# Out-projection of an RWKV block: eight block products per unit, or seven with sums of activations on VectorE

## The chip, the cores and the metric

The kernel runs on one NeuronCore of a Trainium2 chip. Five engines have queues of their own: TensorE (PE; its weight loads are listed as PEld), VectorE (DVE), ScalarE (ACT), GpSimd (POOL) and SyncE (SP), which here only issues transfers. The metric is device time of the core in microseconds, as the median of several runs.

## The reference

The first part is a linear attention with a decaying state, for 4 batches, 8 heads, 768 tokens and head dimension 48. The second part is a feed-forward block on the 3072 tokens with 384 features.

```python
for t in range(S):
    kt, vt, rt, wt = (k[:, :, t], v[:, :, t], r[:, :, t], w[:, :, t])
    cur = np.einsum('bhd,bhe->bhde', u[None] * kt, vt)
    y[:, :, t] = np.einsum('bhd,bhde->bhe', rt, state + cur)
    state = wt[:, :, :, None] * state + np.einsum('bhd,bhe->bhde', kt, vt)
x = attn_out.transpose(0, 2, 1, 3).reshape(B * S, H * D)      # 3072 x 384
h = x @ w_in                                                  # 3072 x 2048
sp = np.maximum(h, 0.0) + np.log1p(np.exp(-np.abs(h)))
g = h * erf(sp)
return (g @ w_out).astype(np.float32)                         # 3072 x 384
```

All of it is fp32.

## The kernel before

The 3072 tokens are cut into 12 units of 256 tokens (NJ = 2 blocks of C = 128 tokens, from two batches). One step of the main loop does the attention of one unit and, between its parts, feed-forward work of earlier units. A unit goes through four stages: attention in step s, the hidden products in step s + 1 (`hidden`, L742), softplus, erf and the product h x erf on ScalarE and VectorE (L724, L727, L731), and the out-projection three steps after its attention (`project`, L771).

The hidden layer of a unit lies in two tiles h (the two halves of the 2048 features), each of 128 partitions x 8 feature blocks x 256 tokens. In `project` each feature block of 128 x 128 is the stationary operand and the 384 columns of w_out are the moving one: 16 feature blocks x 2 token blocks = 32 matmuls of 384 columns per unit. Both token blocks' sums lie in PSUM tiles m from a pool of two (`ps_m`), which the hidden products use too. ScalarE copies each finished sum (L780), and SP sends it out (L781).

Attention inside a step works by levels. At level n the products of neighbouring stretches of 2^(n-1) tokens are taken (`level_products`, L444), VectorE puts them into `own` (L456 and L418), and r and k are scaled by the running decays (`scale`, L260). The first four steps do all levels this way. From step DIRECT = 4 on, distances within blocks of 16 tokens are taken elementwise instead: `prepare` of the next step multiplies shifted rows of r, k and w ("terms", L374, L378, L393) and sums them (L364). VectorE does distances 0 to 4, GpSimd the others (both have L374 and L378). Those steps run `attend_late`, and only the products of the two highest levels are left to PE, at its start and after `place(1)`.

The order of work is written out by hand: every engine runs its instructions in the order of the program. `place(n)` inside the attention calls `in_order`, which takes pieces by letters: P is a piece of the out-projection of unit s - 3, H a piece of the hidden products of unit s - 1, A the next activation (`advance`).

```python
order = ("APPPAPP", "APPP", "HH", "AHHH", "AHHH", "PPAPP")
if s == DIRECT:
    order = ("APPP", "APPP", "APPHH", "AHHH", "AHHH")
```

In a step of `attend_late` the sequence is: level-5 products, scaling and take; the rest of the step before (`from_own`, `through_state`, L478 and L504); the first two parts of `prepare(s + 1)`; the product of kT with its decays (L586); `place(0)`; the next part of `prepare`, and so on. After the last step there remain the out-projections of units 9 to 11 and the hidden products of unit 11.

The weights come as 64-bit numbers and are turned into fp32 in the first three steps and the beginning of the fourth (`convert`): raw words land in tiles `words`, ScalarE splits them, VectorE shifts and joins (L217, L225), GpSimd adds the low part (L229). The same pool `words` later holds rows of r and k (`load_rows`, L178) and part of the terms; `rest` holds rows of w.

Of the kernel before, what the change touches and what calls it, by code (L numbers as in the profile page):

```python
# [11 lines left out]
FP32 = mybir.dt.float32  # L12
I32 = mybir.dt.int32
U32 = mybir.dt.uint32
AF = mybir.ActivationFunctionType
ALU = mybir.AluOpType

P = 128
# [3 lines left out]
NJ = 2  # L22
# [18 lines left out]
NEAR = 1 << NEAR_LOG  # L41
LOG = 6
MASKED = 5


def view(ap, offset, dims):
# [14 lines left out]
def kernel(  # L61
# [30 lines left out]
    const = ctx.enter_context(tc.tile_pool(name="const", bufs=1))  # L92
    ins = ctx.enter_context(tc.tile_pool(name="ins", bufs=2))
    att = ctx.enter_context(tc.tile_pool(name="att", bufs=2))
    xs = ctx.enter_context(tc.tile_pool(name="xs", bufs=3))
    hid = ctx.enter_context(tc.tile_pool(name="hid", bufs=4))
    act = ctx.enter_context(tc.tile_pool(name="act", bufs=2))
    wide = ctx.enter_context(tc.tile_pool(name="wide", bufs=4))
    outs = ctx.enter_context(tc.tile_pool(name="outs", bufs=2))
    dram = ctx.enter_context(tc.tile_pool(name="dram", bufs=2, space=bass.MemoryType.DRAM))  # L100
    ps_p = ctx.enter_context(tc.tile_pool(name="ps_p", bufs=1, space=PSUM))
    ps_y = ctx.enter_context(tc.tile_pool(name="ps_y", bufs=1, space=PSUM))
# [18 lines left out]
    u_row = const.tile([P, D], FP32, name="u_row")  # L121
    w_in_sb = const.tile([P, NT, DM], FP32, name="w_in_sb")
    w_out_sb = const.tile([P, NT, DM], FP32, name="w_out_sb")
    y = ps_y.tile([P, NE, NJ, NP // 2, C], FP32, name="y")

    turns = {"next": 0, "converting": False}
# [44 lines left out]

    def load_rows(s):

        rk = wide.tile([P, 2, DM, 2], I32, name="words", bufs=3)
        rk = rk[:].rearrange("p x n two -> p x (n two)").bitcast(FP32)
        w = wide.tile([P, 2, DM], I32, name="rest", bufs=2)
        w = w[:].rearrange("p x n -> p (x n)").bitcast(FP32)
        nc.sync.dma_start(out=rk, in_=rk_rows[s])  # L178
        nc.sync.dma_start(out=w, in_=w_rows[s])
        rows_of[s] = [x.rearrange("p (t n) -> p t n", t=NEAR) for x in (rk[:, 0], rk[:, 1], w)]  # L180

    def convert(weights):

        held = {}

        def load(i):
            if i >= len(weights):
                return  # L190
            dst, src = weights[i]
            if src.dtype == FP32:
                nc.sync.dma_start(out=dst, in_=src)
                return
            words = wide.tile([P, 2, DM, 2], I32, name="words", bufs=3)
            nc.sync.dma_start(
                out=words[:].rearrange("p i n two -> p i (n two)"), in_=src.bitcast(I32)
            )
            held[i] = [words]

        def scale(i):
            if i in held:
                words = held[i][0]
                low, high = words[:, :, :, 0], words[:, :, :, 1]
                base = ps_p.tile([P, 2, NP * C], FP32, name="pp1")[:, :, :DM]
                rest = wide.tile([P, 2, DM], I32, name="rest", bufs=2)


                nc.scalar.mul(out=base, in_=high.bitcast(FP32), mul=2.0**-112)

                nc.scalar.mul(out=rest[:], in_=low.bitcast(U32), mul=2.0**-29)
                held[i] += [base.bitcast(I32), rest]

        def shift(i):
            if i in held:
                bits = held[i][1]
                nc.vector.tensor_scalar(  # L217
                    out=bits, in0=bits, scalar1=3, scalar2=None, op0=ALU.logical_shift_left
                )

        def join(i):
            if i in held:
                words, bits, rest = held.pop(i)
                into = weights[i][0].bitcast(I32)
                nc.vector.scalar_tensor_tensor(  # L225
                    out=into, in0=words[:, :, :, 1], scalar=-(1 << 31), in1=bits,
                    op0=ALU.bitwise_and, op1=ALU.bitwise_or,
                )
                nc.gpsimd.tensor_tensor(out=into, in0=into, in1=rest[:], op=ALU.add)  # L229

        stages = {"l": load, "s": scale, "h": shift, "o": join}
        done = dict.fromkeys(stages, 0)
        for _ in range(3):
            load(done["l"])
            done["l"] += 1
        while True:
            what = yield
            for stage in {"j": "ho"}.get(what, what):
                stages[stage](done[stage])
                done[stage] += 1  # L240
            if weights[0][1].dtype != FP32:
                turns["converting"] = 0 < done["s"] and done["o"] < len(weights)
                turns["next"] = 0
# [20 lines left out]
    def prepare(s):  # L264
# [75 lines left out]
        r, k, w = rows_of.pop(s)  # L340
        k_rows = k
        front = att.tile([P, 2, JP, C], FP32, name="rk1", bufs=1)
        back = wide.tile([P, 2, DM, 2], I32, name="words", bufs=3)
        front = front[:].rearrange("p x n t -> p (x n t)")
        back = back[:].rearrange("p x n two -> p (x n two)").bitcast(FP32)
        terms, near = {}, 1 << near_log(s)
# [365 lines left out]

    later = []

    def hidden(xT, gs, cut):


        def activate(h):

            held = []  # L720

            def softplus():
                held.append(act.tile([P, FG, UNIT], FP32, name="sp"))
                nc.scalar.activation(held[0][:], h[:], AF.Softplus)  # L724

            def erf():
                nc.scalar.activation(held[0][:], held[0][:], AF.Erf)  # L727

            def multiply():
                for part in (slice(0, FG // 2), slice(FG // 2, FG)):  # L730
                    nc.vector.tensor_mul(h[:, part], h[:, part], held[0][:, part])  # L731

            later.extend([(softplus, True), (erf, True), (multiply, False)])

        for g in range(NG):
            h = hid.tile([P, FG, UNIT], FP32, name="h")
            gs.append(h)
            for f in range(0, FG, FT):
                ps = ps_m.tile([P, FT, UNIT], FP32, name="m")
                for ff in range(FT):  # L740
                    for kk in range(KT):
                        nc.tensor.matmul(  # L742
                            ps[:, ff, :],
                            lhsT=w_in_sb[:, g * FG + f + ff, kk * P : (kk + 1) * P],
                            rhs=xT[:, kk, :],
                            start=kk == 0,
                            stop=kk == KT - 1,
                        )
                    if cut and not ff and g == NG - 1 and f == FG - FT:
                        yield  # L750
                nc.scalar.copy(h[:, f : f + FT, :], ps[:])  # L751
                if f == FG - FT:
                    activate(h)
                yield

    def project(s, gs):

        c, i = divmod(s, SPC)
        ps = [None] * NJ

        halves = [slice(0, FG // 2), slice(FG // 2, FG)]
        for g in range(NG):
            for j, part in (
                [(j, part) for part in halves for j in range(NJ)]
                if not s and g == NG - 1
                else [(j, part) for j in range(NJ) for part in halves]
            ):
                if not g and not part.start:
                    ps[j] = ps_m.tile([P, DM], FP32, name="m")
                for f in range(FG)[part]:  # L770
                    nc.tensor.matmul(  # L771
                        ps[j][:],
                        lhsT=gs[g][:, f, j * C : (j + 1) * C],
                        rhs=w_out_sb[:, g * FG + f, :],
                        start=g + f == 0,
                        stop=g == NG - 1 and f == FG - 1,
                    )
                    if g == NG - 1 and f == FG - 1:
                        o = outs.tile([P, DM], FP32, name="o")
                        nc.scalar.copy(o[:], ps[j][:])  # L780
                        nc.sync.dma_start(out=out[i * NJ + j, c], in_=o[:])  # L781
                    if f % 4 == 3:
                        yield

    xTs, hids, projs = {}, {}, {}
    gated = [[] for _ in range(n_steps)]
# [19 lines left out]
    def piece(kind, of):  # L806
        if not 0 <= of < n_steps:
            return
        if of not in kind:
            kind[of] = hidden(xTs[of], gated[of], not of) if kind is hids else project(of, gated[of])  # L810
        next(kind[of])

    def in_order(s, k):


        order = ("APPPAPP", "APPP", "HH", "AHHH", "AHHH", "PPAPP")
        if s == DIRECT:
            order = ("APPP", "APPP", "APPHH", "AHHH", "AHHH")
        for what in order[k]:
# [27 lines left out]
    with tc.manual_schedule(  # L847
# [16 lines left out]
            ]  # L864
        )
        next(conversion)
        load_step(1)
        for s in range(n_steps):
            xTs[s] = xs.tile([P, KT, UNIT], FP32, name="xT")
# [5 lines left out]
                        conversion.send(what)  # L875

            def place(n):
                if n == (LOG - 1 if s <= DIRECT else 2) and DIRECT - 1 <= s < n_steps - 2:
                    load_rows(s + 2)
                for due in {(3, 4): (5,), (4, 3): (6,), (4, 5): (7,)}.get((s, n), ()):  # L880
                    load_w(due)
# [1 line left out]
                    load_w(s + 3)  # L883
                if s >= DIRECT:
                    in_order(s, next(places))
                    return
                if s in ALONE:
                    if s == 2 and not n:

# [131 lines left out]
```

## Time and profile before

| | |
|---|---|
| median of 3 runs | 616.82 us (616.64 to 618.1) |
| profiled execution, span from first to last instruction | 614.9 us |
| PE busy | 602.1 us (98%) |
| DVE busy | 409.3 us (67%) |
| ACT busy | 293.9 us (48%) |
| POOL busy | 293.3 us (48%) |
| out-projection L771 on PE | 252.1 us |
| hidden products L742 on PE | 257.3 us |
| mean granted TensorE clock | 1.000 |

Durations below come from the one profiled execution, whose span is 1.9 us under the median. A group's line gives the line of code, engine and operation, then the tiles as written <- read, the shapes, the count, and after the bar the busy time in us with the mean duration of one in ns; after the second bar stands the idle time ahead of them and what ended it. Durations of matmuls overlap, so that the mean of one is longer than its share of the busy time. In a timeline each row gives the start in us, the length, the engine, the line and the operation, and in brackets the idle time ahead.

### The profile page before, as it was taken

The page shows a single profiled execution, that of the slowest core. Times are in us where ns is not written, and L with a number is a line of the kernel's source. Part 1 is how long each engine was busy: PE and PEld are TensorE (multiplying, and loading weights), DVE is VectorE, ACT ScalarE, POOL GpSimd, SP SyncE. Part 2 cuts the span into 40 slices and gives each one's busy share as a digit, 9 for nine tenths or more (in the row PEclk, how much of TensorE's full clock was granted, in tenths as well). Part 3 has the DMA queues.
Part 4 walks back from the last instruction along what each step waited for, and adds up shares of the span by engine and source line. Part 5 has one row for each costly group of instructions (what it writes and reads, how often), then busy time and mean ns, then how long its engine had stood idle before and what let it go on. Part 6 is the DMA issues. An engine that isn't in the chain of part 4 may idle for free.

```text
span 614.9 us, 15592 instructions
## 1 busy us (share of the span) xinstructions
PE 602.1 (98%) x6858; PEld 445.9 (73%) x6858; DVE 409.3 (67%) x459; ACT 293.9 (48%) x374; POOL 293.3 (48%) x295
## 2 busy tenths in 40 slices
PE   7889999999999999999999999999999999999997
PEld 6668787678668668668668768768768768668654
DVE  5687696995995897897797797797797311110300
ACT  2548888544446724534534534534534444624600
POOL 4348184603497399299199299299296000000000
PEclk9999999999999999999999999999999999999999
DMA  8376471440353316307307306405303100000000
GB/s 325 117 281 203 184 258 58 164 149 8 136 157 78 101 34 190 112 29 206 101 30 197 109 31 181 126 31 156 117 28 79 25 26 0 9 26 1 0 27 26
DMA packets 51371, 63.27 MB, mean 103 GB/s; under 512 B 34920, under 2 KB 40296, under 8 KB 49896
## 3 DMA queue, kind: packets, MB, share of 16 engines
q1 hardware_dynamic: 50152, 61.68, 31.5%
q8 instruction: 54, 0.88, 0.6%
q10 hardware_dynamic: 1152, 0.59, 0.4%
q14 instruction: 13, 0.11, 0.1%
HBM read 52.39 MB, written 8.69 MB: 99 GB/s over the span
## 4 chain that ended last, share of the span: by engine, by line
PE 85%; DVE 6%; DMA 3%; POOL 2%; issue 2%; ACT 1%; SPq 0%; POOLq 0%; ACTq 0%; DVEq 0%
PE m L771 38%; PE m L742 37%; PE pp L444 4%; DMA w<-in_rkw 3%; PE y L478 2%; PE y L504 1%; PE pp L530 1%; DVE in L260 1%; POOL w_in_sb L229 1%; DVE w_in_sb L225 1%; POOL tot_sb L312 1%; PE pp L673 1%; DVE sums L364 1%; DVE pp L217 1%; DVE own L456 1%
## 5 line engine op out<-in xcount | busy, mean ns | idle before, releaser
L742 PE MATMUL m<-xT,w_in_sb 128*128 128x256 f32 x1152 | 257.3, 382 | 2.4 <-DVE w_in_sb L225 1.2
L771 PE MATMUL m<-w_out_sb,h 128*128 128x384 f32 x768 | 252.1, 488 | 0.0
L742 PEld LDWEIGHTS m<-xT,w_in_sb 128*128 128x128 f32 x1152 | 216.1, 190 | 34.8 <-issue 3.6
L771 PEld LDWEIGHTS m<-w_out_sb,h 128*128 128x128 f32 x768 | 144.6, 190 | 98.5
L751 ACT COPY h<-m 128x512 f32<-128x512 f32 x96 | 56.1, 584 | 130.5 <-PE m L742 130.4
L731 DVE TENSOR_TENSOR h<-h,sp 128x1024 f32<-128x1024 f32 x48 | 74.6, 1594 | 52.1 <-ACT sp L727 51.9
L260 DVE TENSOR_TENSOR in<-in,tot_sb 128x1024 f32<-128x1024 f32 (+1 forms) x60 | 84.4, 1414 | 30.6 <-PE pp L444 27.3
L378 POOL TENSOR_TENSOR words<-words,rest 128x528 f32<-128x528 f32 (+10 forms) x77 | 85.7, 1113 | 6.0
L374 POOL TENSOR_TENSOR rk<-words 128x528 f32<-128x528 f32 (+3 forms) x28 | 44.5, 1588 | 81.2 <-DVE sums L364 70.8
L780 ACT COPY o<-m 128x384 f32<-128x384 f32 x24 | 11.5, 480 | 110.3 <-PE m L771 110.3
L312 POOL TENSOR_TENSOR tot_sb<-tot_sb 128x256 f32<-128x256 f32 (+4 forms) x60 | 54.6, 911 | 4.5
L727 ACT ACTIVATE sp<-sp 128x2048 f32<-128x2048 f32 x24 | 45.9, 1911 | 0.3
L724 ACT ACTIVATE sp<-h 128x2048 f32<-128x2048 f32 x24 | 45.9, 1911 | 0.3
L444 PEld LDWEIGHTS pp<-in 48*64 48x64 f32 (+1 forms) x2368 | 33.8, 125 | 16.3 <-issue 8.5
L364 DVE TENSOR_REDUCE sums<-words 128x6 f32<-128x288 f32 (+8 forms) x66 | 29.2, 470 | 19.4 <-POOL words L374 19.2
L444 PE MATMUL pp<-in 48*64 48x64 f32 (+1 forms) x2368 | 38.3, 212 | 3.7 <-issue 1.6
L727 ACT ACT_TABLE_LOAD x24 | 30.8, 1283 | 15.9 <-issue 13.0
L374 POOL TENSOR_TENSOR words<-words 128x336 f32<-128x336 f32 (+6 forms) x49 | 35.1, 716 | 3.8
L364 DVE TENSOR_REDUCE sums<-rk 128x14 f32<-128x672 f32 (+9 forms) x54 | 34.8, 704 | 0.2
L724 ACT ACT_TABLE_LOAD x24 | 30.8, 1283 | 4.9 <-issue 4.5
L378 DVE TENSOR_TENSOR words<-words,rest 128x576 f32<-128x576 f32 (+8 forms) x34 | 27.9, 820 | 1.2
L229 POOL TENSOR_TENSOR w_out_sb<-w_out_sb,rest 128x768 int32<-128x768 int32 x8 | 17.8, 2222 | 17.8 <-DVE w_out_sb L225 17.7
(80 smaller groups left out, 438.0 us busy)
## 6 DMA issues: line engine op xcount, KB each, us to landing
in<-in_rkw SPq DMA_DIRECT2D x11, 1024.0 KB, 5.6
words<-in_moe_w_in SPq DMA_DIRECT2D x8, 768.0 KB, 4.5
words<-in_moe_w_out SPq DMA_DIRECT2D x8, 768.0 KB, 4.3
words<-in_rk_rows SPq DMA_DIRECT2D x8, 768.0 KB, 6.8
w<-in_rkw SPq DMA_DIRECT2D x11, 512.0 KB, 8.4
v<-in_v SPq DMA_DIRECT2D x12, 384.0 KB, 6.9
out<-o SPq DMA_DIRECT2D x24, 192.0 KB, 1.9
rest<-in_w_rows SPq DMA_DIRECT2D x8, 384.0 KB, 7.3
```

The costliest lines, as they stand in the source:

```text
L260: nc.vector.tensor_mul(halves, halves, view(tots[level - 1], 0, [[1, n], [2, nb], [0, half]]))
L312: nc.gpsimd.tensor_mul(new, pair[:, :, 0], pair[:, :, 1])
L364: nc.vector.tensor_reduce(out=view(sums[:], n, [[near * (NEAR + 1), NEAR // near], [NEAR + 1, near - n]]), in_=terms[n], axis=mybir.AxisLi ...
L374: engine.tensor_mul(terms[n], r[:, :, n:], k[:, :, : near - n])
L378: engine.tensor_mul(k[:, :, :m], k[:, :, :m], w[:, :, n : n + m])
L444: nc.tensor.matmul(pp[s0 : s0 + m, e, n, :m], lhsT=rk[rows(e), 1, n, s0 : s0 + m], rhs=rk[rows(e), 0, n, t0 : t0 + m], start=True, stop=True,)
L724: nc.scalar.activation(held[0][:], h[:], AF.Softplus)
L727: nc.scalar.activation(held[0][:], held[0][:], AF.Erf)
L731: nc.vector.tensor_mul(h[:, part], h[:, part], held[0][:, part])
L742: nc.tensor.matmul(ps[:, ff, :], lhsT=w_in_sb[:, g * FG + f + ff, kk * P : (kk + 1) * P], rhs=xT[:, kk, :], start=kk == 0, stop=kk == KT - 1,)
L751: nc.scalar.copy(h[:, f : f + FT, :], ps[:])
L771: nc.tensor.matmul(ps[j][:], lhsT=gs[g][:, f, j * C : (j + 1) * C], rhs=w_out_sb[:, g * FG + f, :], start=g + f == 0, stop=g == NG - 1 and ...
```

## The change

From unit FAST = 2 on, `project_fast` takes the place of `project`. The product of a unit is seen as a 2 x 2 block product: a11 and a21 are the token blocks in the first h tile, a12 and a22 those in the second; b11, b12 (upper) and b21, b22 (lower) are quarters of w_out with 192 columns. With Winograd's form of Strassen's scheme the four result blocks come from seven products of eight matmuls with 192 columns each:

- sums of activations s1 = a21 + a22, s2 = s1 - a11, s3 = a11 - a21 (over a21's room) are made on VectorE by `blend_halves`, queued behind the second h x erf of the unit; s4 = a12 - s2 is made inside `project_fast`, into the room of s1;
- sums of weights t3, t2, t4 and t1 (over b12's room) are made once on GpSimd by `mix_weights`, three in step 3 and one in step 4;
- products accumulate in two PSUM tiles m0 and m1; three copies on ScalarE and two adds on VectorE per unit make the output tile o.

A unit now has seven pieces P instead of eight, so one P is dropped from the second part of the order. Two tiles are added (`mixed` for the sums of weights, `blend` for s1 and s2), and to make room the pools xs, outs, `words` and `rest` lose a buffer each, and the rows of step s + 2 are loaded later: at place 3 instead of 2, and at place LOG in step 4. The conversion uses the three tiles of `mixed` and one `words` as rooms for raw words, and `blend` for the low parts.

```diff
-    xs = ctx.enter_context(tc.tile_pool(name="xs", bufs=3))
+    xs = ctx.enter_context(tc.tile_pool(name="xs", bufs=2))
...
-    outs = ctx.enter_context(tc.tile_pool(name="outs", bufs=2))
+    outs = ctx.enter_context(tc.tile_pool(name="outs", bufs=1))
...
+    mixed = const.tile([P, 3, FG, ND], FP32, name="mixed")
+    blend = const.tile([P, 2, FG, C], FP32, name="blend")
...
-        rk = wide.tile([P, 2, DM, 2], I32, name="words", bufs=3)
+        rk = wide.tile([P, 2, DM, 2], I32, name="words", bufs=2)
...
-        w = wide.tile([P, 2, DM], I32, name="rest", bufs=2)
+        w = wide.tile([P, 2, DM], I32, name="rest", bufs=1)
...
+            def blend_halves():
+                (a11, a21), (a12, a22) = [[g[:, :, j * C : (j + 1) * C] for j in range(NJ)] for g in gs]
+                s1, s2 = blend[:, 0], blend[:, 1]
+                nc.vector.tensor_add(s1, a21, a22)
+                nc.vector.tensor_sub(s2, s1, a11)
+                nc.vector.tensor_sub(a21, a11, a21)
+
             later.extend([(softplus, True), (erf, True), (multiply, False)])
+            if fast and len(gs) == NG:
+                later.append((blend_halves, False))
...
+    def mix_weights():
...
+        nc.gpsimd.tensor_tensor(out=t3, in0=b22, in1=b12, op=ALU.subtract)
+        yield
+        nc.gpsimd.tensor_tensor(out=t2, in0=t3, in1=b11, op=ALU.add)
+        yield
+        nc.gpsimd.tensor_tensor(out=t4, in0=b21, in1=t2, op=ALU.subtract)
+        yield
+        nc.gpsimd.tensor_tensor(out=b12, in0=b12, in1=b11, op=ALU.subtract)
+        yield
+
+    def project_fast(s, gs):
...
+        a11, a12 = (g[:, :, :C] for g in gs)
+        s3, a22 = (g[:, :, C:] for g in gs)
+        s1, s2 = blend[:, 0], blend[:, 1]
+        s4 = s1
...
+        def product(to, a, b, start):
+            for f in range(FG):
+                nc.tensor.matmul(
+                    to, lhsT=a[:, f], rhs=b[:, f], start=start and f == 0, stop=f == FG - 1,
+                    skip_group_check=True,
+                )
+
+        product(m0[:, lo], a11, b11, True)
+        nc.scalar.copy(o[:, 0, lo], m0[:, lo])
+        yield
+        product(m1[:, lo], a22, t4, True)
+        yield
+        product(m1[:, hi], s1, t1, False)
+        nc.scalar.copy(o[:, 1], m1[:])
+        nc.vector.tensor_sub(s4, a12, s2)
+        yield
+        product(m0[:, lo], s2, t2, False)
+        nc.scalar.copy(o[:, 0, hi], m0[:, lo])
+        yield
+        product(m1[:, hi], s4, b22, False)
+        yield
+        product(m0[:, lo], s3, t3, False)
+        nc.vector.tensor_add(
+            o[:, 1].rearrange("p (k n) -> p k n", k=2), o[:, 1].rearrange("p (k n) -> p k n", k=2),
+            m0[:, None, lo].to_broadcast([P, 2, ND]),
+        )
+        nc.sync.dma_start(out=out[i * NJ + 1, c], in_=o[:, 1])
+        yield
+        product(m1[:, lo], a12, b21, True)
+        nc.vector.tensor_add(o[:, 0], o[:, 0], m1[:])
+        nc.sync.dma_start(out=out[i * NJ, c], in_=o[:, 0])
+        yield
...
-        order = ("APPPAPP", "APPP", "HH", "AHHH", "AHHH", "PPAPP")
+        order = ("APPPAPP", "APP", "HH", "AHHH", "AHHH", "PPAPP")
...
-                if n == (LOG - 1 if s <= DIRECT else 2) and DIRECT - 1 <= s < n_steps - 2:
+                if n == {DIRECT - 1: LOG - 1, DIRECT: LOG}.get(s, 3) and DIRECT - 1 <= s < n_steps - 2:
                     load_rows(s + 2)
...
                 if s >= DIRECT:
                     in_order(s, next(places))
+                    if s == DIRECT and n == LOG - 1:
+                        next(mixing)
                     return
+                if s == DIRECT - 1 and LOG - 2 <= n <= LOG:
+                    next(mixing)
```

## The prediction

> **What bounds the kernel now.** I read the engine totals first, then the two matmul groups, then the stretches of single steps. On the page:
>
> ```profile
> PE 602.1 (98%) x6858; PEld 445.9 (73%) x6858; DVE 409.3 (67%) x459; ACT 293.9 (48%) x374; POOL 293.3 (48%) x295
> L742 PE MATMUL m<-xT,w_in_sb 128*128 128x256 f32 x1152 | 257.3, 382 | 2.4 <-DVE w_in_sb L225 1.2
> L771 PE MATMUL m<-w_out_sb,h 128*128 128x384 f32 x768 | 252.1, 488 | 0.0
> ```
>
> PE is never free, and the out-projection (L771) is 41% of the span. Each fp32 matmul is two records, so 12 units x 32 matmuls give x768: 252.1/768 = 0.328 us of PE per record (starts of single records: 0.3225 apart). One number from a whole run hides the stages, so I cut it at the steps (columns: stretch, length, then busy time of PE, PEld, DVE, ACT, POOL):
>
> ```profile
> 343.89:390.17 46.28, 46.28 (x492) 34.59 (x485) 38.94 (x46) 20.80 (x25) 32.06 (x33) 1.00 0.37 112
> 483.01:531.17 48.16, 48.16 (x400) 35.05 (x393) 9.11 (x12) 23.86 (x26) 0.00 (x0) 1.00 0.04 11
> 531.17:614.90 83.73, 80.32 (x286) 53.11 (x280) 8.53 (x8) 27.81 (x30) 0.00 (x0) 1.00 0.05 16
> ```
>
> There are two regimes. In a middle step (5 to 10; the first row is step 7) PE has no gap, but VectorE is already 84% busy. In step 11 and the tail VectorE is nearly idle. A saving of PE work is real in both, and VectorE work is only cheap in the second.
>
> **Is a 192-column pass really half a 384-column one?** Weight loads last 190 ns, so a 192-column stream (160 ns) could be held up by them. The warm-up matmuls (128 columns, full weights) answer it, cold and warm, in the stretches for L852; beside them the keep-busy matmuls by shape:
>
> ```profile
> 5.80:7.80 2.00, 2.00 (x21) 2.00 (x20) 1.00 1.04 382
> 2.20:5.20 3.00, 3.00 (x16) 3.00 (x15) 1.00 0.91 260
> ```
> ```profile
> L631 PE MATMUL y<-s,ident 128*128 128x384 f32 x12 | 5.5, 538 | 0.0
> L631 PE MATMUL y<-s,ident 128*128 128x192 f32 x12 | 2.9, 326 | 0.0
> ```
>
> Warm records start 112 ns apart although each needs a full load; so loads cost no more than 112 ns. The 192-column pairs: 2.9/6 less one duration of 0.326 leaves 0.157; the single starts are 0.161 apart. I take 0.161.
>
> **What the Trainium skill says.** "TensorE: Matmul & The Clock Gate", "Step-by-step: what each phase is for": weights of the next matmul load while this one runs. The trace agrees (112 against 190 ns). Same page, "Architectural detail: the array is 16× 32×32, not 1× 128×128": VectorE's and ScalarE's queues are strict FIFO; nothing in this trace contradicts it. Same page, "Part 1: The HAM clock gate": after an idle window of some 3.4 us TensorE falls to half clock and needs a busy window to recover. The trace has the cold start (213 ns per start until 5.5 us, 112 after) but no later PE gap of that length, so the fall is not shown here. "SBUF — State Buffer", "Who interferes with whom": a VectorE instruction with two SBUF inputs and a GpSimd instruction that reads SBUF block each other for a whole instruction. The trace agrees; from the timelines of VectorE and of GpSimd:
>
> ```profile
> 118.34 2.25 DVE L378 TENSOR_TENSOR words<-words,rest 128x576 f32<-128x576 f32 x1
> ```
> ```profile
> 117.56 2.41 POOL L229 TENSOR_TENSOR w_out_sb<-w_out_sb,rest 128x768 int32<-128x768 int32 x1
> ```
>
> The 576-element product takes 0.76 when GpSimd is quiet, and 1024-element ones take 1.2 alone and 2.12 beside GpSimd.
>
> **The change, part by part.**
>
> *PE work.* Per unit 64 passes x 0.3225 = 20.64 become 112 x 0.161 = 18.06: -2.58. Units 2 to 11, ten of them: -25.8.
>
> *VectorE work.* Per unit four 128x1024 sums (1.2 to 2.2 each) and two 128x384 adds from PSUM (L604, 48x384 from PSUM: 0.55). That is 6 to 10 us into a 46-us step with 7.3 us idle.
>
> *The new wait.* This decides. The fifth product, s4 x b22, needs s4 = a12 - s2, which VectorE makes into the buffer of s1. In the order of instructions, s4 stands on VectorE behind the whole first half of the next step's block terms. VectorE of step 7, timeline (P starts at 343.89):
>
> ```profile
> 342.69 1.23 DVE L260 TENSOR_TENSOR in<-in,tot_sb 128x1024 f32<-128x1024 f32 x1 [0.77 <-PE pp L444]
> ...
> 344.43 0.95 DVE L381 TENSOR_TENSOR words<-words,u_row 128x768 f32<-128x768 f32 x1
> ...
> 356.91 1.73 DVE L586 TENSOR_TENSOR kT<-kT,spread 128x768 f32<-128x768 f32 x1
> 358.56 4.26 DVE L731 TENSOR_TENSOR h<-h,sp 128x1024 f32<-128x1024 f32 x2
> ```
>
> The new instruction goes between the last two. The chain cannot start earlier: its first instruction waits for PE's level-5 products, the last thing before P. So s4 starts 14.7 us after P starts and, at 2.12 beside GpSimd, ends at 16.8 to 16.9. PE has done four products by 4 x 16 x 0.161 = 10.3. It stands still for 6.6 us. By the same reading (end of L586 after P's start, plus 2.12 and 0.1 for the signal): step 6 13.6, so 5.5; steps 7 to 9 14.75, so 6.6 each; step 10 14.4, so 6.3; step 5 16.2, so 8.1. Sum 39.7. PE's three remaining products, then everything after, are late by it.
>
> *Step 5 in addition.* In step 4 GpSimd gets t1 = b12 - b11 ahead of `faded` (L682): 1536 elements at 1.31/528 (L374, alone), about 3.5 us. VectorE's `middle` add waits for `faded`, then h multiplies, then the first three sums (about 4). VectorE has 1.7 us to spare there, so it enters step 5 some 5.4 late: +5.4 on its stall. Bounds 2 and 7.
>
> *Step 3.* Three more 1536-element sums run on GpSimd from 120 on, while VectorE works through two-input products that PE's next levels wait for. Each can hold VectorE for 3.5 us; VectorE has about 1.3 us before PE's level 5 waits. Bounds 0 and 9; I take 5. (GpSimd itself was idle from 121 to 148.)
>
> *Behind s4.* Queued on VectorE are two h multiplies (4.26), a product with w (2.12), two scalings (3.7), and only then the adds that free PSUM buffers m0 and m1: 16.9 + 10.1 + 0.55 gives m0 at 27.5. PE ends P at 16.9 + 7.75 + 0.2, does level 6 and the state (1.65 before) and wants m0 at 26.4 to 26.5: a stall of 1.1 to 1.2. Over six steps 7.2. Later things fit: own (L418), 40.8 to 42 after P's start before, comes at about 47; the hidden products end at 48.5.
>
> *Clock.* A gap of 6.6 us holds a whole idle window nine times in ten by the skill's window. Then P5 to P7 run at half clock for about 4.5 us (the cold start here took 3.8), which costs 2.25 and swallows the m0 wait: together H starts 2.45 later instead of 1.2. Six steps: 14.7 in place of 7.2. Bounds 7 and 20.
>
> *Step 11 and the tail* (units 8 to 11). No block terms stand ahead of s4; it follows the third product by 1.2, against 2.58 of fourth product. No stall; the -2.58 are kept four times, already counted.
>
> *Edits at nothing.* ScalarE's third PSUM copy (+0.3 per unit, 48% busy). The output transfers now wait for VectorE (28 instead of 16 and 21), ahead of g_rows and spread on SP's queue, which are wanted 13 us into the next step. The rows of step s+2 are loaded behind by_tokens, issued at about 39 and landing 7 us later (6.8 to 7.3 by the page), wanted at 52; without that cover of 5 us, lateness would go straight into s4. The weights' conversion gets four rooms instead of three: bounded by -2 and +1, taken as 0.
>
> *Sum.* 614.9 - 25.8 + 39.7 + 5.4 + 5 + 14.7 = 653.9 for the profiled execution. The median stands 1.9 above its span: 655.8, rounded to 655.
>
> **The rivals.**
>
> *Full clock after the stall*: as above with 7.2 for 14.7: 648. Part of the same case; the range holds both.
>
> *VectorE is bound by its sum, not by the order*, if it ran ahead enough to have s4 ready: 38.9 + 4 x 1.7 + 1.1 + 2.9 of waits for PE at the fence = 49.7 per step, +3.4 six times, -10.3 for the last four units, +5 in step 3: 632. Against it: the fence (L487) makes VectorE wait for PE 2.1 us each step.
>
> *Faster: PE's gain is kept everywhere.* One mechanism: s4 is ready when the fourth product ends, less than 10.3 us after P starts. Then 616.8 - 25.8 + 1 = 592. For it: PE is the bound and 112-ns starts are shown. Against it: 14.7 us of measured VectorE work stand before s4. It decides only if at least 6 us of these are elsewhere in the changed order, and they are not.
>
> *Weight loads set the pace*, so that the change doesn't shorten PE work: 112 x 0.19 = 21.3 per unit, +0.64 ten times instead of -2.58, stalls shorter by 1.8 six times: 677. Against it the 112 ns above.
>
> **How the numbers follow.** Stall at s4, either clock: 0.86. VectorE's sum: 0.05. PE's gain kept: 0.05. Weight loads: 0.04. Low end: s4 at 1.2 (-5.5), step 3 at 1, step 5 at 2, full clock: 635. High end: step 3 at 9, long cold stretches (+5.3): 664; I take 668 for a wait at the rows. Under 2 in 10 lie outside. A difference under 0.3% is no change here. Faster 0.05, within 0.01, slower 0.94.
>
> **What would show it.** In the changed profile: PE idle 5 to 7 us before the fifth product in steps 5 to 10, released by VectorE; more in step 5; none in the last four units, whose out-projections take 18.1 us; steps of 51 to 53 us; the granted clock below 1 after the gaps if the skill's window holds; PE waits around 125 to 133. Wrong if s4 stands earlier than 10 us, if records of 192 columns start 0.19 apart, or if the rows come late.

## The result and the profile after

The changed kernel takes 663.84 us (median of 4 runs, 662.42 to 666.91) against 616.73 for the kernel before (4 runs): 1.0759 times as long, with a 95% interval of 1.0727 to 1.0791. The forecast was 655 (635 to 668). The profiled execution took 664.59, of which 662.8 are its span; the span before was 614.9, so 47.9 us have to be accounted for.

From the page of the changed kernel: engine totals, TensorE's granted clock in 40 slices (tenths of full speed), and one group of the new products.

```profile
PE 597.2 (90%) x7338; PEld 523.7 (79%) x7338; DVE 476.3 (72%) x519; ACT 293.4 (44%) x384; POOL 333.2 (50%) x299
...
PEclk9999999969999969979979998997998999999999
...
L834 PE MATMUL m<-w_out_sb,blend 128*128 128x192 f32 x320 | 68.9, 379 | 40.6 <-DVE blend L846 40.6
```

PE was 98% busy and is now 90% busy, and its clock is no longer full everywhere (mean 0.955). The last line says where: ahead of the products of s1 and s4 PE sat idle for 40.6 us, all of it until VectorE's s4 (L846) was made. The view of waits gives the number of times and the longest:

```profile
PE m L834 <- DVE blend L846: 40.6, 6, 12.3
```

Six waits, one for each of steps 5 to 10; none in the last four units. Now the stretches (columns as before: length, then busy PE, PEld, DVE, ACT, POOL, clock, DMA share, GB/s), a piece of step 3, then steps 8 and 11 and the tail. The stretch at 343.89 that the prediction calls step 7 is step 8 by the count (320 of the 768 records of L771 lie ahead of it); its sum takes the same stall for both, so nothing in it depends on that name.

```profile
126.20:136.40 10.20, 2.26 (x11) 0.99 (x10) 10.10 (x6) 0.65 (x2) 8.57 (x3) 0.81 0.28 91
381.32:435.08 53.76, 46.22 (x539) 42.70 (x533) 46.31 (x54) 20.73 (x26) 35.74 (x33) 0.94 0.33 96
...
540.60:586.30 45.70, 45.70 (x450) 42.25 (x448) 12.55 (x15) 24.00 (x28) 0.00 (x0) 1.00 0.04 12
586.30:662.80 76.50, 73.00 (x424) 70.21 (x416) 23.25 (x23) 27.65 (x32) 0.00 (x0) 0.99 0.05 17
```

Step 8 grew from 46.28 to 53.76, while step 11 fell from 48.15 to 45.7 and the tail from 83.74 to 76.5. Inside step 8, first TensorE's timeline and then VectorE's (start, length, instruction, idle time ahead; P starts at 381.32):

```profile
386.62 2.76 PE L834 MATMUL m<-w_out_sb,blend 128*128 128x192 f32 x16
389.22 2.76 PE L834 MATMUL m<-mixed,blend 128*128 128x192 f32 x16
398.31 4.72 PE L834 MATMUL m<-w_out_sb,blend 128*128 128x192 f32 x16 [6.33 <-DVE blend L846]
```
```profile
394.33 1.69 DVE L594 TENSOR_TENSOR kT<-kT,spread 128x768 f32<-128x768 f32 x1
395.95 2.22 DVE L846 TENSOR_TENSOR blend<-h,blend 128x1024 f32<-128x1024 f32 x1
398.09 4.16 DVE L739 TENSOR_TENSOR h<-h,sp 128x1024 f32<-128x1024 f32 x2
```

Products start 2.60 us apart (16 x 0.161 = 2.58), the fourth is over at 392.0, and the fifth starts at 398.31, just after s4 has ended (395.95 + 2.22 = 398.17). s4 starts 14.63 us after P, against 14.7 predicted from VectorE's order. The fifth product takes 4.72 instead of 2.76: the clock has fallen.

In step 3 the three sums of weights (timelines of GpSimd, then of VectorE, then of TensorE):

```profile
122.05 3.83 POOL L808 TENSOR_TENSOR mixed<-w_out_sb 128x1536 f32<-128x1536 f32 x1
125.95 3.81 POOL L810 TENSOR_TENSOR mixed<-mixed,w_out_sb 128x1536 f32<-128x1536 f32 x1
...
130.94 3.83 POOL L812 TENSOR_TENSOR mixed<-w_out_sb,mixed 128x1536 f32<-128x1536 f32 x1
```
```profile
122.62 3.87 DVE L382 TENSOR_TENSOR rk<-words 128x576 f32<-128x576 f32 x1
126.52 3.76 DVE L386 TENSOR_TENSOR words<-words,rest 128x480 f32<-128x480 f32 x1
...
131.53 3.65 DVE L386 TENSOR_TENSOR words<-words,rest 128x384 f32<-128x384 f32 x1
```
```profile
136.37 1.99 PE L452 MATMUL pp<-in 48*64 48x64 f32 x64 [7.94 <-DVE in L268]
```

Each sum on GpSimd holds one product on VectorE until it ends: three products that took 1.27, 0.66 and 0.56 us before last 3.87, 3.76 and 3.65, and PE waits 7.94 us for the scaling behind them. The clock falls in this gap too (0.81 on average in the stretch above).

The 47.9 us by steps (spans of the profiled executions):

| part | before | after | measured | predicted |
|---|---|---|---|---|
| steps 0 to 2 | 100.57 | 102.57 | +2.0 | 0 |
| step 3 | 52.75 | 63.76 | +11.0 | +5.0 |
| step 4 | 49.49 | 49.5 | 0.0 | 0 |
| steps 5 to 10 | 280.2 | 324.76 | +44.6 | +44.3 |
| step 11 and tail | 131.89 | 122.22 | -9.7 | -10.3 |
| sum | 614.9 | 662.8 | +47.9 | +39.0 |

The predicted +44.3 is -15.5 of PE work, 39.7 + 5.4 of stalls and 14.7 for the clock and m0. That it meets the measured +44.6 so closely is luck in part: the stalls came out about 3 us shorter, and gaps of about 3 us that the prediction did not have made up for it (below).

### The profile page after: what moved, and what is told of

It is laid out like the page before. It is cut to its first block, busy times and chain, and to the rows that moved or that the text cites. A ratio compares the mean times of both kernels' runs of the same rounds, so it can differ in the third digit from the quotient of the medians.

```text
span 662.8 us, 16667 instructions
## 1 busy us (share of the span) xinstructions
PE 597.2 (90%) x7338; PEld 523.7 (79%) x7338; DVE 476.3 (72%) x519; ACT 293.4 (44%) x384; POOL 333.2 (50%) x299
## 4 chain that ended last, share of the span: by engine, by line
PE 60%; DVE 27%; issue 4%; POOL 4%; DMA 3%; ACT 1%; SPq 0%; DVEq 0%; POOLq 0%; ACTq 0%
PE m L759 32%; PE m L834 20%; DVE words L386 5%; DVE sums L372 4%; PE pp L452 4%; DVE rk L382 4%; DMA w<-in_rkw 3%; DVE in L268 3%; DVE blend L846 2%; DVE h L739 2%; DVE own L464 2%; DVE kT L594 1%; PE y L486 1%; PE pp L538 1%; DVE words L389 1%
## 5 line engine op out<-in xcount | busy, mean ns | idle before, releaser
L834 PE MATMUL m<-w_out_sb,blend 128*128 128x192 f32 x320 | 68.9, 379 | 40.6 <-DVE blend L846 40.6
L834 PEld LDWEIGHTS m<-w_out_sb,blend 128*128 128x128 f32 x320 | 64.7, 227 | 42.2 <-issue 37.0
L268 DVE TENSOR_TENSOR in<-in,tot_sb 128x1024 f32<-128x1024 f32 (+1 forms) x60 | 81.0, 1350 | 19.0 <-PE pp L452 14.9
L386 POOL TENSOR_TENSOR words<-words,rest 128x528 f32<-128x528 f32 (+10 forms) x77 | 89.2, 1158 | 6.0
L320 POOL TENSOR_TENSOR tot_sb<-tot_sb 128x256 f32<-128x256 f32 (+4 forms) x60 | 59.4, 990 | 4.5
L834 PE MATMUL m<-mixed,h 128*128 128x192 f32 x320 | 56.2, 330 | 0.0
L834 PE MATMUL m<-w_out_sb,h 128*128 128x192 f32 x320 | 55.9, 329 | 0.0
L834 PEld LDWEIGHTS m<-mixed,h 128*128 128x128 f32 x320 | 53.8, 194 | 0.1
L834 PEld LDWEIGHTS m<-w_out_sb,h 128*128 128x128 f32 x320 | 52.1, 190 | 0.7
L452 PE MATMUL pp<-in 48*64 48x64 f32 (+1 forms) x2368 | 39.7, 215 | 12.8 <-DVE in L268 9.2
L846 DVE TENSOR_TENSOR blend<-h,blend 128x1024 f32<-128x1024 f32 x10 | 18.2, 1819 | 40.8 <-PE m L834 40.8
L788 PE MATMUL m<-w_out_sb,h 128*128 128x384 f32 x128 | 43.2, 492 | 0.0
```

The source lines that it names most:

```text
L268: nc.vector.tensor_mul(halves, halves, view(tots[level - 1], 0, [[1, n], [2, nb], [0, half]]))
L320: nc.gpsimd.tensor_mul(new, pair[:, :, 0], pair[:, :, 1])
L386: engine.tensor_mul(k[:, :, :m], k[:, :, :m], w[:, :, n : n + m])
L452: nc.tensor.matmul(pp[s0 : s0 + m, e, n, :m], lhsT=rk[rows(e), 1, n, s0 : s0 + m], rhs=rk[rows(e), 0, n, t0 : t0 + m], start=True, stop=True,)
L788: nc.tensor.matmul(ps[j][:], lhsT=gs[g][:, f, j * C : (j + 1) * C], rhs=w_out_sb[:, g * FG + f, :], start=g + f == 0, stop=g == NG - 1 and ...
L834: nc.tensor.matmul(to, lhsT=a[:, f], rhs=b[:, f], start=start and f == 0, stop=f == FG - 1, skip_group_check=True,)
```

## The experiments

**The theory**: s4 is late by its place in VectorE's queue; PE's stall costs the clock too; the sums of weights in step 3 cost the rest. The rivals: VectorE is too busy whatever the order; the changed surroundings (pools, later rows) cost by themselves; seven products bring nothing.

**Without three sums of weights.** t3, t2 and t4 are left out, and the products take b22, b11 and b21 in their places, so part of the computation is missing.

```diff
-        nc.gpsimd.tensor_tensor(out=t3, in0=b22, in1=b12, op=ALU.subtract)
         yield
-        nc.gpsimd.tensor_tensor(out=t2, in0=t3, in1=b11, op=ALU.add)
         yield
-        nc.gpsimd.tensor_tensor(out=t4, in0=b21, in1=t2, op=ALU.subtract)
...
-        t3, t2, t4 = (mixed[:, n] for n in range(3))
+        t3, t2, t4 = b22, b11, b21
```

> Leaves out the three sums of weights t3, t2, t4 on GpSimd in step 3; the products take b22, b11 and b21 in their place, so part of the out-projection isn't computed. Theory (the three sums on GpSimd, 3.8 us each, hold VectorE's two-input products in step 3 and PE behind them): step 3 falls from 63.8 back to 52.9 us, 11 us less in all, 653 us. Rival (step 3 is late through the later loads and the fewer buffers): step 3 stays at 63 to 64, 664 us.

Measured: 652.79 us, 1.0563 (1.0532 to 1.0595; a ratio is always to the kernel before), 11.05 less than the change. Step 3 is 52.75 us long, as before the change. The 11 us of step 3 come from these three instructions.

**The fifth product last, a12 x b21 into the upper half of m0.** The order becomes P1, P2, P3, P4, P6, P7, P5.

```diff
-        product(m1[:, hi], s4, b22, False)
-        yield
         product(m0[:, lo], s3, t3, False)
...
-        product(m1[:, lo], a12, b21, True)
-        nc.vector.tensor_add(o[:, 0], o[:, 0], m1[:])
+        product(m0[:, hi], a12, b21, True)
+        nc.vector.tensor_add(o[:, 0, lo], o[:, 0, lo], m0[:, hi])
+        yield
+        product(m1[:, hi], s4, b22, False)
+        nc.vector.tensor_add(o[:, 0, hi], o[:, 0, hi], m1[:, hi])
...
-        order = ("APPPAPP", "APP", "HH", "AHHH", "AHHH", "PPAPP")
+        order = ("APPPAPPPP", "A", "HH", "AHHH", "AHHH", "PPAPPPP")
```

> The product with s4 goes to the end of the unit (order P1 P2 P3 P4 P6 P7 P5, P7 into the unused half of m0), and all seven pieces and the adds into o go ahead of the second part of the preparation; the same sums, products and copies, one add split in two. Theory (the place of the waits in VectorE's order costs the time, not the amount of its work alone): PE's product with s4 is due at 15.5 us after P starts and s4 ready at 16.9, so the gap of 6.6 us shrinks to 1.4, m0 is free at 22, the clock stays near 1, and a step of the middle takes 48.9 us instead of 52 to 54, now set by VectorE (its last sum for the next step ends 46.0 after P starts, and 2.9 us of PE follow). Six steps: 27 us less, 637 us. Rival (VectorE's added work alone sets the step): steps stay at 52 to 54, 664 us. Rival (PE keeps its gain once the wait is gone): steps of 43.7 to 45, 612 us.

Measured: 685.49 us, 1.1093 (1.1054 to 1.1131). A miss: it is slower than the change, not faster. TensorE's timeline in step 8 of this kernel:

```profile
398.51 2.87 PE L834 MATMUL m<-mixed,h 128*128 128x192 f32 x16 [1.40 <-ACT o L849]
407.92 4.53 PE L834 MATMUL m<-w_out_sb,h 128*128 128x192 f32 x13 [6.54 <-DVE o L852]
```

The wait for s4 is gone, but a12 x b21 now writes the tile m0 that the first add into o (L852) reads, and that add stands on VectorE behind s4 and two products h x erf. So the edit exchanged one wait behind s4 for another, and added a wait of 1.4 us for ScalarE's copy. In the last four units PE waits too (step 11 and tail 133.3 against 122.2). The run says nothing on the theory itself; the last but one below does the same thing without this wait.

**Only the surroundings.** The changed pools, tiles, conversion rooms, order of the rows and output tile, but eight products for every unit (FAST = 99) and no sums. The surroundings hold one more edit, which the diff of the change above does not show: `dynamic_dma_scratch_size=1024` where the program is made. No run separates it.

```diff
-FAST = 2
+FAST = 99
...
-        order = ("APPPAPP", "APP", "HH", "AHHH", "AHHH", "PPAPP")
+        order = ("APPPAPP", "APPP", "HH", "AHHH", "AHHH", "PPAPP")
...
-                    if s == DIRECT and n == LOG - 1:
-                        next(mixing)
...
-                if s == DIRECT - 1 and LOG - 2 <= n <= LOG:
-                    next(mixing)
```

> Only the surroundings of the change: fewer buffers, other rooms for the conversion, later loads of the rows, but every unit goes through the old out-projection and no sums of weights or activations are made. Theory: steps 3 to 11 as before (middle steps 46.3 us), the first three steps 2 us later as in the changed kernel: 618 to 619 us. Rival (the later row loads or the smaller pools hold the block terms): middle steps over 47 us, over 624 us. Rival (the 2 us are chance): 617 us.

Measured: 624.74 us (6 runs), 1.0112 (1.0091 to 1.0133). A miss: the surroundings, which the prediction took at nothing, cost 7.5 us. Steps 5, 6, 9 and 10 are 50.21, 47.97, 48.45 and 47.94 long against 48.48, 46.32, 46.57 and 46.27. The largest single loss is a gap of 2.67 us in the state products of step 5, put down to "issue": no semaphore is waited for. Step 9 has another, of 1.86 us. Steps 6 and 10 have none; there the granted clock is 0.50 for 3.41 us, from 0.8 to 1.6 us after the end of the gap before. Step 0 is 1.7 us longer, with a gap of 2.15 us (0.95 before) and again 3.4 us at clock 0.50.

**Only the later rows.** The kernel before, with the loads of step s + 2 moved as in the change.

```diff
-                if n == (LOG - 1 if s <= DIRECT else 2) and DIRECT - 1 <= s < n_steps - 2:
+                if n == {DIRECT - 1: LOG - 1, DIRECT: LOG}.get(s, 3) and DIRECT - 1 <= s < n_steps - 2:
                     load_rows(s + 2)
```

> The kernel before with one edit: the rows of step s + 2 are loaded at place 3 (at place LOG in step 4), as in the change; all buffers, rooms and products as before. Theory (the later transfer lies over the moment when PE fetches its next instructions, and PE stands in the state products of steps 5, 6, 9 and 10 for 1 to 2.7 us with no wait of the program): those four steps are about 1.7 us longer each, 623 to 625 us, as with all the surroundings. Rival (the smaller pools or the conversion's rooms cost the 7.5 us): 617 us.

Measured: 622.74 us (6 runs), 1.009 (1.0063 to 1.0117): 5.5 of the 7.5 us. TensorE's timeline at the same place, first in the kernel before, then in this one:

```profile
250.92 0.44 PE L504 MATMUL y<-in,middle 48*48 48x64 f32 x16 [0.94 <-issue]
```
```profile
249.40 0.40 PE L504 MATMUL y<-in,middle 48*48 48x64 f32 x16
252.80 0.44 PE L504 MATMUL y<-in,middle 48*48 48x64 f32 x16 [3.00 <-issue]
```

The trace's queue of instruction fetches (q8) points to the reason. In the kernel before, a block of 16384 bytes is fetched at 248.6, takes 0.96, and PE has a gap of 0.94 until 250.92. With the later rows, 1.2 MB are moved between 246 and 250.1, the fetch starts only as they end, takes 1.26, and PE goes on at 252.80. In the surroundings alone it starts at 251.8, again as the transfers end, takes 1.36, and PE goes on at 254.50. In all three PE goes on 1.3 to 1.5 us after the fetch has ended. So the fetch seems to wait behind the data, and PE for the fetch; that is read from the order in time, and no run moves the fetch alone. The Trainium skill, "Runtime: NRT & Kernel Launch", "Instruction fetch mechanics", says that instructions come in blocks of 16 KiB over a DMA queue of the engine's own, with a cost at each boundary that is mostly hidden. The traces agree: the kernel before has 54 such fetches and three gaps above 0.5 us that are put down to "issue". With the row transfers ahead of the fetches, the gap of 0.94 grew to 3.00 and one of 1.60 came up in step 9.

The gaps are not the whole cost. Of the 5.2 us in this profiled execution step 5 has 2.1 and step 9 has 1.6, by the gaps; step 6 has 1.65 with no gap, for the clock is at half behind the gap of step 5 (a stretch of it, columns as before, clock third from the end):

```profile
253.42:256.83 3.41, 3.41 (x6) 1.75 (x6) 3.27 (x5) 1.30 (x5) 0.00 (x0) 0.50 0.10 24
```

Of the six runs the one with a mean clock of 1.000 took 620.07 us and the three at 0.991 and 0.992 took 623.59 to 625.15: it seems that the same gaps cost more where the clock falls behind them (only one of the six left a trace). In the profiled execution of the surroundings, steps 0, 5, 6, 9 and 10, which hold these gaps and stretches, make up 8.6 of the 8.7 us by which it is longer.

**Seven products only for the last three units**, in the changed surroundings; the sums of weights are made in step 11.

```diff
-FAST = 2
+FAST = 9
...
-                    if s == DIRECT and n == LOG - 1:
+                    if s == n_steps - 1 and n:
                         next(mixing)
...
```

> The seven products only for the last three units (9 to 11), which run after the block terms are over; the sums of weights are made in step 11, where GpSimd and VectorE are idle. Theory (PE's saving of 2.58 us a unit is real where VectorE is free): 7.6 us less than the run with the surroundings alone, 611 us, faster than before. Rival (weight loads or copies eat the saving also there): 618 us.

Measured: 617.36 us (14 runs), 0.9994 (0.9974 to 1.0014). The rival that seven products bring nothing is out: against the surroundings alone it is 7.4 us faster, and the tail went from 83.69 to 76.5, that is -7.19 for three units (2.40 each; the prediction had 2.58). The surroundings eat this gain.

**PE kept busy in the gap.** 16 more matmuls into the unused half of m0, after the fourth product, in units 2 to 7. They add work that no output uses.

```diff
         nc.scalar.copy(o[:, 0, hi], m0[:, lo])
+        if s < n_steps - 4:
+            for f in range(16):
+                nc.tensor.matmul(
+                    m0[:, hi], lhsT=a11[:, f % FG], rhs=b11[:, f % FG], start=False, stop=True,
+                    skip_group_check=True,
+                )
```

> In units 2 to 7, after the fourth product, sixteen matmuls of 192 columns whose result nobody reads go into the unused half of m0; they take 5.2 us of the gap of 6.4. Theory (the idle gap halves TensorE's clock, and the three products after it pay 1.9 to 3.2 us each step, 14.9 in all): the granted clock stays at 1, the three products take 7.8 us again, and PE then waits about 0.7 for m0: 10 to 11 us less, 653 us. Rival (the slow products are due to waits for PSUM or VectorE, not to the clock): 664 us or more.

Measured: 656.41 us, 1.0631 (1.0608 to 1.0653): 7.4 less than the change, though PE does more. The fillers and then the fifth product, in TensorE's timeline of step 8 (P starts at 378.4):

```profile
390.44 5.47 PE L852 MATMUL m<-w_out_sb,h 128*128 128x192 f32 x32 [1.40 <-ACT o L849]
395.74 2.76 PE L834 MATMUL m<-w_out_sb,blend 128*128 128x192 f32 x16
```

The fifth product takes 2.76 again instead of 4.72, and the hidden products begin 27.2 us after P instead of 28.5. The mean clock is 0.987 instead of 0.955. So the half clock costs 7.4 us of the time here, against the 7.5 by which the prediction's 14.7 exceeds its 7.2. My expectation of 10 to 11 overlooked that at full clock PE comes earlier to the wait for m0 (0.21 left), and that the fillers let the fifth product start 0.35 us later (17.34 after P instead of 16.99).

**s4 made early**, with the other sums, over a12. The last product then takes s4 in place of a12, so its result is changed.

```diff
                 nc.vector.tensor_sub(a21, a11, a21)
+                nc.vector.tensor_sub(a12, a12, s2)
...
-        s4 = s1
+        s4 = a12
...
-        nc.vector.tensor_sub(s4, a12, s2)
```

> s4 is made right after s3, at the end of the step before, over a12; nothing of it stands between the block terms and the fifth product any more. The seventh product then takes s4 in place of a12, so the output isn't the reference's. Theory (s4 is only the first of two waits on VectorE's order; behind it stands m0, which the hidden products take over and which is freed by an add 25 us after P starts): no gap before the fifth product, a gap of about 5 us before the hidden products instead, still with a halved clock after it; steps of 50 to 51 us instead of 52 to 54, 648 to 652 us. Rival (s4's wait was the whole cost): steps of 46 to 47, 625 us.

Measured: 656.82 us (two runs, 654.0 and 659.7), 1.0629 (1.0497 to 1.076). No gap above 0.5 us is left inside P. From the view of waits:

```profile
PE m L760 <- DVE o L854: 30.5, 6, 9.6
```

PE now runs through all seven products and waits before the hidden products for the add that frees m0: 5.25 us in steps 6 to 8. Steps 6 to 10 are 50.1 to 52.9 long. The prediction's "m0 wait behind s4" is there, and taking s4 away only uncovers it: the wait belongs to the place in VectorE's queue, not to s4. That the gain would come back with s4 early is refuted.

**The fifth product last, with a12 x b21 fourth**, before m0 has a reader in the way. The activations come later, and the adds into o ahead of the second part of the preparation.

```diff
         nc.vector.tensor_sub(s4, a12, s2)
         yield
+        product(m0[:, hi], a12, b21, False)
+        yield
         product(m0[:, lo], s2, t2, False)
...
+        nc.vector.tensor_add(o[:, 0, lo], o[:, 0, lo], m0[:, hi])
...
-        product(m1[:, lo], a12, b21, True)
-        nc.vector.tensor_add(o[:, 0], o[:, 0], m1[:])
+        product(m1[:, hi], s4, b22, False)
+        nc.vector.tensor_add(o[:, 0, hi], o[:, 0, hi], m1[:, hi])
...
-        order = ("APPPAPP", "APP", "HH", "AHHH", "AHHH", "PPAPP")
+        order = ("APPPPPAPP", "A", "HH", "AHHH", "AHHH", "PPAPPPP")
```

> The product with s4 last, now in an order that leaves no other wait ahead of it: P1 P2 P3, then a12 b21 into the free half of m0, then P4, P6 and at the end P5; the activation stages move behind P4, all adds into o ahead of the second part of the preparation. Theory (the places in VectorE's order cost the time): gap before the last product about 1 us, m0 free 22 us after P starts, no halved clock, VectorE's sum sets the step: 48.9 us, up to 1.5 more where instructions are fetched late; 637 to 644 us. Rival (the amount of VectorE's work): steps stay at 52 to 54, 664 us.

Measured: 635.2 us, 1.0287 (1.0265 to 1.0309): 28.6 less than the change, with the same seven products and the same sums on VectorE (one add is split in two). Steps 6 to 10 are 46.56, 48.87, 48.24, 47.93 and 45.75 long. The gap in P is gone except in step 5 (6.32), and another wait appears at the end of the step, in TensorE's timeline:

```profile
459.19 1.16 PE L452 MATMUL pp<-in 48*64 48x64 f32 x64 [1.78 <-DVE in L268]
```

PE waits for VectorE's last scaling. This is the rival "VectorE is bound by its sum": in the change it is hidden under the wait for s4, and it shows as soon as the order is mended. It is 1.38 to 1.79 us in steps 6 to 9, and in two of them the clock is at 0.50 for 3.41 us behind it; a wait of 0.41 us for ScalarE's copy comes on top. So the middle steps do not get their 2.58 us back even then.

**Seven products where VectorE is idle.** The kernel before, with its pools and rows untouched; seven products only for units 9 to 11. The sums of weights lie in the three `words` tiles, s1 and s2 in rk1, which are free once step 11's terms are made, in step 10.

```diff
+FAST = 9
...
+    def borrow():
+
+        lent["blend"] = att.tile([P, 2, JP, C], FP32, name="rk1", bufs=1)
+        lent["mixed"] = [
+            wide.tile([P, 2, DM, 2], I32, name="words", bufs=3)[:]
+            .rearrange("p i n two -> p (i n two)").bitcast(FP32).rearrange("p (f n) -> p f n", f=FG)
+            for _ in range(3)
+        ]
...
+            kind[of] = hidden(xTs[of], gated[of], not of, of >= FAST) if kind is hids else (
+                project_fast if of >= FAST else project
+            )(of, gated[of])
...
+                    if s == n_steps - 1 and not n:
+                        borrow()
                     in_order(s, next(places))
+                    if s == n_steps - 1 and n:
+                        next(mixing)
```

> The kernel before with the seven products for the last three units alone; the sums of weights and activations lie in the tiles of the block terms (words, rk1), which are free after step 10, so that no pool, room or row load changes. Theory (2.4 us a unit are gained where VectorE is free, and the surroundings cost what the gain brings): the tail as in the run with the last three units, 76.5 us instead of 83.7, all before it as in the kernel before: 609 to 610 us, ratio 0.988. Rival (the gain needs the other surroundings, or PE's instruction fetch eats it): 615 to 617 us.

Measured: 611.11 us (5 runs, 610.61 to 612.6), 0.990 (0.9884 to 0.9915): 1% faster than the kernel before. PE is busy for 98% of the span again. The stretch of its tail:

```profile
532.80:609.30 76.50, 73.03 (x425) 70.21 (x416) 23.25 (x23) 27.65 (x32) 0.00 (x0) 1.00 0.05 18
```

The tail lost 7.2 us and the clock stayed full. Step 10 grew by 1.2 (47.47 against 46.27); a gap of 0.98 stands there before the products of `own`, and VectorE's steps ahead of it (the scaling and the product for `own`, 1024 elements each) lasted 4.47 and 4.46 us, beside sums of 4.43 and 4.31 on GpSimd.

## Why the prediction was right, and where it was off

*PE work: right.* 192-column records start 0.161 apart, and step 11 and the tail got 9.7 of the 10.3 us. (112 x 0.161 is 18.03 and not 18.06, which changes nothing.)

*The new wait: right.* s4 ends 16.85 us after P in step 8 (16.8 to 16.9 predicted). Counted from when the fifth product was due (10.4 us after P, which is about 0.25 ahead of the gap, for a record outlasts its turn), the six stalls are 12.5, 6.6, 6.6, 6.6, 5.1 and 4.7: 42.1 us against 45.1. Step 6 was sized 1.1 too low: s4 ends 16.85 us after P there as well. Steps 9 and 10 were sized too high; the reason stands below under the edits at nothing. Early s4 moved the wait to m0, and s4 last without a reader in the way took 28.6 us off: both place the cause in VectorE's order.

*Step 5 in addition: right.* 12.5 against 8.1 + 5.4 = 13.5. The sum t1 lasted 3.45 us (3.5 predicted), and VectorE waited for `faded` behind it, where before it had waited 1.93 us for PE:

```profile
209.12 1.13 DVE L709 TENSOR_TENSOR middle<-faded,pp 48x384 f32<-48x384 f32 x2 [4.37 <-POOL faded L690]
```

*Clock and m0: right.* The fifth to seventh products of the six steps last 10.6, 9.7, 10.9, 9.85, 11.0 and 9.65 us against 7.8 at full clock: +14.9 (14.7 predicted), and no gap is left before the hidden products. The Trainium skill, "TensorE: Matmul & The Clock Gate", "Part 1: The HAM clock gate", has the fall after an idle window of some 3.4 us. Here six gaps of 4.46 to 12.25 us each have a slow product behind them. But the clock also fell behind shorter gaps: 3.00 us with the later rows, 2.67 in the surroundings alone, 1.78 in the reordering with a12 x b21 fourth. So a gap as long as that window is not needed here. In the change itself the gaps of 1.14 to 1.57 us had no half clock behind them.

*Step 3: mechanism right, size off.* 11.0 us, outside the bounds of 0 and 9. The "about 3.5 us" for each sum was a slip (1536 x 1.31/528 is 3.81, and the sums measured 3.81 to 3.83), but the 5 did not follow from it either: it was a value picked between bounds, and two terms were missing. The four products from 122.6 on (3.87, 3.76, 1.17, 3.65) took 1.27, 0.66, 0.66 and 0.56 before: 9.3 more, less the 1.3 of slack, is 8.0, against 7.94 measured. This sum was not made in the prediction. Nor was the clock after this gap added, as it had been for s4: level 5 took 1.99 instead of 1.16, and the hidden products behind it 7.62 instead of 5.45, 3.0 us together.

*Edits at nothing: one was wrong, in the kernel before.* "The rows of step s + 2 are loaded behind by_tokens" was looked at only for being late at VectorE; they were not. With this edit alone the kernel before takes 5.5 us more, in gaps of PE behind instruction fetches and in half clock behind the gaps. What the later rows cost in the change itself is not shown. There, gaps of the same kind stand in steps 8, 9 and 10 (1.22, 1.57 and 1.14 us), behind fetches that ended 1.4 to 1.5 us before PE went on. But no other transfer lay over these three fetches or in the 2.5 us ahead of them, so row transfers do not explain them; the kernel before has its gap of 0.94 with nothing over the fetch, too. What makes PE run into a fetch there stays open. The first two gaps came out of the stalls of the next steps, for PE reached P later and s4 no later: 6.6 - 1.2 = 5.4 and 6.3 - 1.6 = 4.7, against 5.1 and 4.7 measured. Only the gap of step 10 has no stall behind it. Together: -15.5 of PE work, 42.1 of stalls, 14.9 of clock and 3.9 of these gaps, less 0.9 that the kernel before had in step 5, is 44.5, against 44.6 measured.

*Steps 0 to 2*: +2.0, not foreseen. 0.9 of it are two gaps at 15 and 22 us (1.33 and 1.17 against 0.95 and 0.62), behind instruction fetches again. The seven kernels above with the same code there take 31.3 to 32.9 for step 0, the change 32.5, so this part varies from one execution to another. The rest stays open.

The rivals: "full clock after the stall" (648) is refuted by the clock, "PE's gain is kept everywhere" and "weight loads set the pace" by the gaps and the 0.161. "VectorE is bound by its sum" does not hold in the change, but it is the next limit once the order is mended.

## What to carry to other kernels

Work taken off the engine that bounds a kernel is a gain only if what replaces it arrives in time, and that is read from its place in the helper's in-order queue (start and length of everything ahead of it), not from the helper's busy share. Where an operand is late, look for the next wait behind the same queue before moving it: here early s4 and one reordering each met another wait, and only an order with no reader of m0 in the way paid. The same transformation gave 1% where the helper was idle and tiles could be borrowed, without touching pools or transfers elsewhere. A gap on TensorE can cost more than its length: read the granted clock of the stretch behind it as well.

## What the runs showed of the hardware

A two-input sum of 1536 elements on GpSimd (3.8 us) held two-input products on VectorE until it ended, three times of three in step 3. The Trainium skill, "SBUF — State Buffer", "Who interferes with whom", says that the two block each other for a whole instruction; here that made a product of 0.56 us last 3.65.

Every gap on PE of 2.15 us and more in these traces was followed by a stretch at half clock; behind the gaps of 4.46 us and more in the change the next product took 4.5 to 5.5 us instead of 2.76. Shorter gaps went both ways: half clock behind 1.86 us (surroundings alone) and 1.78 us (a12 x b21 fourth, step 7), none behind 1.60 us (later rows) and 1.40 us (first reordering, next product 2.87). The short ones with half clock behind them stand next to small products of the attention; whether that matters, no run separates. Apart from the first and the last, the stretches at half clock were 3.41 us long or a multiple of it.

PE stood still behind some of its instruction fetches, for 0.6 to 3.0 us, with no semaphore that explains it, and went on 1.2 to 1.6 us after the fetch had ended. The longest of these gaps (2.67 and 3.00 us) had transfers of over 1 MB ending as the fetch began; those of 1.14 to 1.57 us in the change had none near.
